# A fused attention and soft-MoE kernel: first q and k turned in the scores' banks, row maxima half a slot later, negated maxima ahead of load issues

## The chip, the cores and the metric

The kernel runs on one core of a Trainium2 chip. The metric is device time in microseconds (us). The engines are named as in the profile: PE (TensorE matmuls, with PEld for its weight loads), DVE (VectorE), ACT (ScalarE), POOL (GpSimd), SP (SyncE). DMAs are issued from GpSimd's queue for all inputs and from SyncE's queue for the output.

## The reference

```python
def _attn_ref(q, k, v):                    # q, k, v: (8, 12, 448, 64)
    scale = 1.0 / np.sqrt(q.shape[-1])
    scores = scale * np.matmul(q, k.transpose(0, 1, 3, 2))
    m = np.max(scores, axis=-1, keepdims=True)
    e = np.exp(scores - m)
    attn = e / (np.sum(e, axis=-1, keepdims=True) + np.exp(-m) + 1e-09)
    return np.matmul(attn, v)

def _moe_ref(x, phi, w1, w2):              # x: (3584, 768), 8 experts of 4 slots, F = 1024
    logits = x @ phi
    d = np.exp(logits - logits.max(0, keepdims=True)); d /= d.sum(0, keepdims=True) + 1e-09
    slot_input = (d.T @ x).reshape(E, S_per_e, D)
    slot_out[e] = np.maximum(slot_input[e] @ w1[e], 0.0) @ w2[e]
    c = np.exp(logits - logits.max(1, keepdims=True)); c /= c.sum(1, keepdims=True) + 1e-09
    return c @ slot_out
```

The attention output, with heads put side by side, is the x of the mixture.

## The kernel before

The 96 heads are worked in 48 pairs (`NPAIR`); a pair is two heads of one batch, on partitions 0 to 63 and 64 to 127. Three pairs (`NP`) are one load group of q, k and v, so there are 16 groups (`NG`). The program order of each engine is written out by hand in one loop over slots `s`, one slot for each pair and one more, each of two half slots `y` (`hs = 2 * s + y`).

The steps of a pair n are these.

- `T(n)` turns q and k: 28 transposes on PE into one PSUM tile `ps_t` (L216), then a copy to SBUF, by ACT (L219) for n < 6 and for the first pair of each group, else by DVE (L221). Seven such copies exist in turn (`NQK`).
- `A(n, i)`, a run, computes a quarter of the pair's scores for the row maxima alone: matmuls into `ps_a` (L249, L259, or L240 where they are mixed with other work) and `reduce_max` on DVE (L253, L262, L242). Runs 0 to 2 have a maximum for each head, run 3 (64 rows a head) one for both, so a pair has seven maxima. The list `runs` holds the order of all runs, and `As(c)` takes the next c of them.
- `W1(g)` negates the maxima of a maxima group on GpSimd (L269: three instructions into `wm`, one into `ngm`). Maxima group 0 is pair 0 alone, group 1 is pairs 1 and 2, later ones are three pairs. `W2(g)` turns them by four matmuls into `ps_m` (L289, L290), `W3(g)` copies that to `mT` and makes the exponentials `ec` of the negated maxima (L295 to L301, ACT).
- `Bk(n, i)` computes the scores again, turned, with keys on partitions, adds the negated maximum by a second matmul with `sel` and `mT`, and ACT takes the exponential (L320 to L325 where a run is mixed in, else L349 to L355).
- `V(g)` puts v of a group into place on GpSimd (four copies, L361 to L364). `AV` multiplies the exponentials with v and a column of ones (L386), `N1` evacuates the sums (L398), `N2` divides by the denominators (`rec`, L407, L408 on DVE, L414 to L423 on GpSimd; on DVE for the last four pairs), and `PX` turns the result for the mixture (L444, L450).
- `P(b)` gives the steps of the mixture's routing for one batch, spread over later half slots by the table `post`.

In slot s the loop runs `Bk(s, ..)`, two runs in each half slot (four in half slots 0 to 4, `early`), `T(s + 6)`, or `T(hs + 3)` in the first half slots, `AV(s, ..)` and the late part of `AV(s - 1, ..)`, `N1` and `N2` of s - 1 and `PX(s - 2)`. In every third slot (s % 3 == 2), in the second half, come W2 and W3 of the next maxima group; W1 of that group stands at the end of the slot before.

PSUM has three pools: `psA` with three banks (tag "a": `ps_a`, `ps_t`, the routing's tiles), `psB` with four (tag "b": `ps_b`, `ps_m`, `ps_x`), `psV` with one.

All loads are issued by GpSimd, in the order of the program: q, k and v of later groups (`load`), half matrices of the experts' weights in two DMAs each (`load_half`, at slots given by `half_at`), and the rows of the last five half matrices (`load_rows`, at half slots given by `rows_at`), which go to SBUF that q, k, v and their products have left by then; rows 7 and 8 go to the place of the loaded v. After the loop come the experts' two layers (L741, L755) and the output (L811 to L822).

Of the kernel before, what the change touches and what calls it, by code (L numbers as in the profile page):

```python
# [9 lines left out]
BF16 = mybir.dt.bfloat16  # L10
# [14 lines left out]
HG = 6  # L25
NP = 3
W65 = 65
# [4 lines left out]
def kernel(  # L32
# [10 lines left out]
    nc = tc.nc  # L43
    B, H, S, D = q.shape
# [9 lines left out]
    NPAIR = B * PB  # L54
    NG = NPAIR // NP
# [69 lines left out]
    def load_rows(r0, r1):  # L125

        while r0 < r1:
            i, z = divmod(r0, FK)
            n = min(r1 - r0, FK - z)
            load_part(11 + i, z, z + n)  # L130
            r0 += n

    with ExitStack() as at:
# [33 lines left out]
        load(1, "k")  # L167


        for h in range(2):  # L170
            nc.vector.tensor_add(ident2[:, 64 * h:64 * h + 64], ident[:, 0:64], ident[:, 64:128])
        nc.vector.tensor_copy(identf, ident)
# [6 lines left out]
                pattern=[[-1, HG]], channel_multiplier=1)  # L179

        nc.vector.reduce_max(band, ident.rearrange("p (i s) -> p i s", i=4), axis=AX.X)
# [11 lines left out]
        nc.vector.memset(ones[64:128, 1:2], 0.0)  # L193
        gdma(out=phi_sb, in_=moe_phi.rearrange("(j p) s -> p j s", p=128))

        mx, ngm, ec, mT, eT, av, us = {}, {}, {}, {}, {}, {}, {}
# [8 lines left out]

        def T(n):
            g, pl = divmod(n, NP)
            ps = psA.tile([128, 2, S], BF16, tag="a", name="ps_t")
            for a in range(2):
                src = nat["qk"[a], g]  # L210
                for tok in range(7):
                    for hl in range(2):

                        c = kcol(hl, tok) if a else (2 * tok if tok < 4 else 2 * tok - 7) * 64
                        r = slice(64 * hl, 64 * hl + 64)
                        nc.tensor.transpose(ps[r, a, c:c + 64], src[r, pl, tok * D:(tok + 1) * D], ident[r, r])  # L216
            t = qk_t[n % NQK]
            if n < 6 or pl == 0:
                nc.scalar.copy(t, ps)  # L219
            else:  # L220
                nc.vector.tensor_copy(t, ps)  # L221
            qkT[n] = t
# [377 lines left out]
            post.setdefault(2 * NPAIR - 5 + 2 * z - (z == 3), []).append(last[z])  # L600


        runs = [(n, i) for n in range(NPAIR) for i in range(4)]

        def As(c):
            for _ in range(min(c, len(runs))):
# [14 lines left out]
        As(1)  # L621
        for nm in "qk":
            load(2, nm)

        half_at = {s: i for i, s in enumerate((1, 4, 7, 10, 13, 16, 22, 25, 28, 31, 34))}


        rows_at = {77: 3, 83: 7, 85: 12, 87: 13, 89: 17, 91: 20, 92: 24, 93: 26, 95: 27}  # L630
        rows = 0
        for s in range(NPAIR + 1):
            for y in range(2):
                hs = 2 * s + y
                early = int(hs < 5)
                mix = s >= 3 and len(runs) > 1 and runs[0][1] == 2 * y
                if mix:
                    Bk(s, 2 * y, mix=True)
                    Bk(s, 2 * y + 1, y, mix=True)
                else:  # L640
                    As(1)
                if mix:
                    pass
                elif s < NPAIR:
                    Bk(s, 2 * y)
                    As(early)
                    side = int(y == 1 and len(runs) > 0 and runs[0][1] == 3)
                    Bk(s, 2 * y + 1, side)
                    As(1 - side)
                else:  # L650
                    As(1)
                if hs == 1:
                    W1(1)
                if hs < 5:
                    T(hs + 3)
                if y == 0:
                    if 0 <= s - 1:
                        for i in (2, 3):
                            AV(s - 1, i, range(3))
                else:  # L660
                    if 2 <= s < NPAIR - 6:
                        T(s + 6)
                    g = (s + 1) // 3
                    if (s + 1) % 3 == 0 and g < NG:
                        W2(g + 1)
                        W3(g + 1)
                    if s < NPAIR:
                        for i in (0, 1):
                            AV(s, i, range(3))
                for f in post.get(hs, ()):  # L670
                    f()
                if y and 0 <= s - 2 < NPAIR - 2:
                    PX(s - 2)
                if y == 0:
                    if 0 <= s - 1:
                        for i in range(4):
                            AV(s - 1, i, [3])
                        if s == NPAIR:
                            PX(s - 2)
                        N1(s - 1)  # L680
                        if not on_pool(s - 1):
                            N2(s - 1)
                else:
                    if 0 <= s - 1 and on_pool(s - 1):
                        N2(s - 1)
                As(early)
                if hs == 1:
                    W2(1)
                    W3(1)
                if hs == 4:  # L690
                    W1(2)
                if y == 0 and hs in rows_at:
                    load_rows(rows, rows_at[hs])
                    rows = rows_at[hs]
            g = (s + 10) // 3
            if s == 1 or (s and s % 3 == 2):
                if g < NG:
                    load(g, "q")
                    load(g, "k")
            g = (s + 9) // 3  # L700
            if s % 3 == 0 and g - 2 < NG:
                V(g - 2)
                if s and g - 1 < NG:
                    load(g - 1, "v")
            if s % 3 == 1:
                if 1 < (s + 2) // 3 < NG:
# [146 lines left out]
```

## Time and profile before

| | |
|---|---|
| median of 3 runs | 311.84 us (311.04 to 312.73) |
| profiled execution | 313.42 us |
| its span, first to last instruction | 311.6 us |
| busy: DVE maxima L242, L262, L253 | 135.3, 29.4, 23.7 us (612 to 617 ns each) |
| busy: ACT copies of T (L219), DVE copies of T (L221) | 18.8 us in 20; 17.1 us in 28 |
| DMA, mean over the span | 174 GB/s |

A row of the timeline has the start in us, the duration, engine, line, operation, result and operands, the count of instructions merged into the row and, in brackets, how long the engine had stood before it and what it waited for last. Where several instructions are merged, the duration is from the first's start to the last's end; an instruction's own duration is a little longer than the distance to the next. A row of the table of stretches has the stretch in us, its length, then for PE, PEld, DVE, ACT and POOL the busy time and count, the clock share, the DMA share and GB/s.

### The profile page before, as it was taken

To read this page: it belongs to the slowest core of one execution; us is meant where nothing else is said; L and a number is where in the kernel's file an instruction comes from. 1 tells how busy PE (TensorE), PEld (TensorE's weight loads), DVE (VectorE), ACT (ScalarE), POOL (GpSimd) and SP (SyncE) were. 2 spreads that over 40 slices of the span, in tenths; PEclk is the share of its full clock that TensorE was granted. 3 is DMA by queue.
4 is the path that set the end of the run, shared out by engine and by line. 5 is a ranking of instruction groups with operands and counts; after the bars stand their busy time and mean duration, and the time that the engine had idled before them with its cause. 6 is when DMAs were issued, how large, how long until landed. Compare 5 with 4: busy or idle time off the path is not lost.

```text
span 311.6 us, 12145 instructions
## 1 busy us (share of the span) xinstructions
PE 279.1 (90%) x5070; PEld 160.7 (52%) x5070; DVE 250.9 (81%) x575; ACT 247.4 (79%) x546; POOL 196.9 (63%) x402
## 2 busy tenths in 40 slices
PE   2899899999999999999999999999999996997800
PEld 1444466565566566656556665566655554461100
DVE  4777999999989999998999899989997455237910
ACT  2357499999999999999899999998999984218700
POOL 8642778879878987697979688976776713000000
PEclk9999999999999999999999999999999998697555
DMA  6990399999999999687999999999445999935997
GB/s 86 150 130 12 45 203 207 198 190 169 190 196 166 208 172 208 78 129 126 207 156 187 171 203 154 194 181 160 79 53 103 161 191 210 211 72 214 449 439 312
DMA packets 36934, 54.30 MB, mean 174 GB/s; under 512 B 2576, under 2 KB 27664, under 8 KB 36496
## 3 DMA queue, kind: packets, MB, share of 16 engines
q0 software_dynamic: 35872, 42.52, 84.8%
q1 hardware_dynamic: 1008, 11.01, 8.3%
q8 instruction: 39, 0.64, 0.8%
q14 instruction: 15, 0.12, 0.1%
HBM read 85.03 MB, written 11.01 MB: 308 GB/s over the span
## 4 chain that ended last, share of the span: by engine, by line
PE 68%; DVE 15%; ACT 6%; issue 3%; POOL 3%; POOLq 0%
PE ps_av L386 14%; PE ps_a L240 10%; PE ps_t L216 7%; PE ps_b L320 6%; DVE mx L242 6%; PE ps_b L323 6%; PE ps_b L349 5%; DVE mx L253 3%; PE ps_b L352 3%; PE ps_o L811 3%; PE ps_x L444 3%; PE ps_h L741 2%; PE ps_a L249 2%; PE ps_s L544 2%; ACT W L817 2%
## 5 line engine op out<-in xcount | busy, mean ns | idle before, releaser
L242 DVE TENSOR_REDUCE mx<-ps_a 128x1 f32<-128x448 f32 x246 | 135.3, 612 | 3.3 <-PE ps_a L240 2.6
L325 ACT ACTIVATE W<-ps_b 128x448 bf16<-128x448 f32 x246 | 118.4, 575 | 0.2 <-PE ps_a L240 0.2
L240 PE MATMUL ps_a<-W 64*128 64x448 bf16 x246 | 79.9, 352 | 0.0
L320 PE MATMUL ps_b<-W 64*128 64x448 bf16 x246 | 67.8, 352 | 0.3
L323 PE MATMUL ps_b<-mT,sel 64*128 64x448 bf16 x246 | 65.5, 350 | 0.0
L386 PE MATMUL ps_av<-W 128*128 128x65 bf16 (+1 forms) x1536 | 65.2, 196 | 0.3 <-issue 0.3
L386 PEld LDWEIGHTS <-W 128*128 128x128 bf16 (+1 forms) x1536 | 50.4, 101 | 27.6 <-issue 23.6
L414 POOL TENSOR_TENSOR W<-ubuf,rec 128x384 bf16<-128x384 f32 x44 | 36.2, 823 | 37.8 <-DVE rec L408 24.3
L355 ACT ACTIVATE W<-ps_b 128x448 bf16<-128x448 f32 x90 | 47.5, 568 | 8.0 <-PE ps_b L352 8.0
L216 PEld LDWEIGHTS <-W 64*64 64x64 bf16 x1344 | 31.2, 113 | 19.2 <-issue 8.0
L216 PE MATMUL ps_t<-ident,W 64*64 64x64 bf16 x1344 | 32.1, 198 | 5.8 <-DMA W<-in_q_dram 4.2
L112 POOL DMA_DIRECT2D W<-in_moe_w_dram x37 | 24.7, 669 | 13.7 <-PE ps_s L544 5.1
L450 ACT CAST W<-ps_x 128x512 bf16<-128x512 f32 x47 | 28.1, 599 | 5.9 <-PE ps_x L444 5.7
L262 DVE TENSOR_REDUCE mx<-ps_a 128x1 f32<-128x448 f32 x48 | 29.4, 613 | 0.6 <-PE ps_a L259 0.3
L349 PE MATMUL ps_b<-W 64*64 64x448 bf16 (+1 forms) x138 | 28.9, 380 | 0.1
L240 PEld LDWEIGHTS <-W 64*128 64x128 bf16 x246 | 23.0, 94 | 9.8
L219 ACT COPY W<-ps_t 128x896 bf16<-128x896 bf16 x20 | 18.8, 940 | 11.3 <-PE ps_t L216 11.1
L253 DVE TENSOR_REDUCE mx<-ps_a 128x1 f32<-128x448 f32 x42 | 23.7, 617 | 4.5 <-PE ps_a L249 4.2
L352 PE MATMUL ps_b<-mT,sel 64*64 64x448 bf16 (+1 forms) x138 | 27.0, 362 | 0.0
L323 PEld LDWEIGHTS <-sel 64*128 64x128 bf16 x246 | 20.0, 94 | 12.4 <-issue 2.2
L398 ACT COPY ubuf<-ps_av 128x455 f32<-128x455 f32 x44 | 25.2, 574 | 1.2 <-PE ps_av L386 1.0
L423 POOL TENSOR_TENSOR W<-ubuf,rec 128x128 bf16<-128x128 f32 x44 | 17.5, 398 | 3.7
(133 smaller groups left out, 440.1 us busy)
## 6 DMA issues: line engine op xcount, KB each, us to landing
W<-in_moe_w_dram POOLq DMA_DIRECT2D x25, 768.0 KB, 9.8
out_dram<-W SPq DMA_DIRECT2D x3, 2688.0 KB, 11.1
W<-in_v_dram POOLq DMA_DIRECT2D x32, 192.0 KB, 6.2
W<-in_q_dram POOLq DMA_DIRECT2D x15, 336.0 KB, 6.6
W<-in_k_dram POOLq DMA_DIRECT2D x15, 336.0 KB, 7.4
W<-in_moe_w_dram POOLq DMA_DIRECT2D x5, 576.0 KB, 10.1
out_dram<-W SPq DMA_DIRECT2D x3, 768.0 KB, 4.2
W<-in_moe_w_dram POOLq DMA_DIRECT2D x1, 960.0 KB, 9.7
```

The source lines that it names most:

```text
L216: nc.tensor.transpose(ps[r, a, c:c + 64], src[r, pl, tok * D:(tok + 1) * D], ident[r, r])
L240: nc.tensor.matmul(ps[:, 0:S], t[r, 0, i * 128:(i + 1) * 128], t[r, 1, :], start=True, stop=True)
L242: nc.vector.reduce_max(m[:, c:c + 1], ps[:, 0:S], axis=AX.X)
L253: nc.vector.reduce_max(mx[g][:, c:c + 1], pss[hl][:, 0:S], axis=AX.X)
L320: nc.tensor.matmul(pss[hl][:, 0:S], t[rs[hl], 1, cols], t[rs[hl], 0, :], start=True, stop=False)
L323: nc.tensor.matmul(pss[hl][:, 0:S], sel[rs[hl], 2 * pl + hl:2 * pl + hl + 1].to_broadcast([64, 128]), mT[mg(n)][rs[hl], :], start=False, s ...
L325: nc.scalar.activation(e[:, hl, :], pss[hl][:, 0:S], AF.Exp, scale=scale)
L349: nc.tensor.matmul(outs[hl], t[rs[hl], 1, cols], t[rs[hl], 0, :], start=True, stop=False)
L352: nc.tensor.matmul(outs[hl], sel[rs[hl], 2 * pl + hl:2 * pl + hl + 1].to_broadcast([64, m]), mT[mg(n)][rs[hl], :], start=False, stop=True)
L355: nc.scalar.activation(e, p[:, 0:S], AF.Exp, scale=scale)
L386: nc.tensor.matmul(o, eT[n, i, hl][:, qc], vp[g % 2][:, 2 * pl + hl, i, 0:W65], start=(i == 0 and u == 0 and hl == 0), stop=(i == 3), skip ...
L414: eng.tensor_mul(x[:, 0:3, c:c + 128].rearrange("p i (h d) -> p i h d", h=2), u[:, 0:6, 0:D].rearrange("p (i h) d -> p i h d", h=2), rec[: ...
```

## The change

- **Setup.** The work on the identity (`ident2`, `identf`, `sel`, `band`) moves behind the memsets on DVE. The order on GpSimd stays.
- **T.** For the first nine pairs `ps_t` is in `psB`. The copy of T(0) is split: q by ACT, k by DVE. The copies of T(7) and T(8) move from DVE to ACT.
- **Runs.** The order in a pair is 0, 3, 1, 2. Half slot 4 takes two runs in place of four, so that all later maxima are taken half a slot later and the last two runs lie in slot 44.
- **W1.** From group 2 on, W1 stands at the end of the first half of the slot in whose second half W2 stands. The order on GpSimd stays, other than in slots 1, 2 and 44.
- **Weight loads.** Half matrix 0 is loaded ahead of the loop, the others a step earlier up to slot 13, then at slots 19, 22, 28, 31 and 34 (before: 16, 22, 25, 28, 31 and 34). The first DMA of a half and `load(2, "v")` stand behind W1.
- **The end.** V(15) moves from the end of slot 42 to slot 44, behind W1(16) and ahead of N2(43), and with it the loads of rows 7 and 8; row 12 is loaded half a slot later.

```diff
         def T(n):
             g, pl = divmod(n, NP)
-            ps = psA.tile([128, 2, S], BF16, tag="a", name="ps_t")
+            first = n < NP * NP
+            ps = (psB if first else psA).tile([128, 2, S], BF16, tag="b" if first else "a", name="ps_t")
...
             t = qk_t[n % NQK]
-            if n < 6 or pl == 0:
+            if n == 0:
+                nc.scalar.copy(t[:, 0, :], ps[:, 0, :])
+                nc.vector.tensor_copy(t[:, 1, :], ps[:, 1, :])
+            elif first or pl == 0:
                 nc.scalar.copy(t, ps)
...
-        runs = [(n, i) for n in range(NPAIR) for i in range(4)]
+        runs = [(n, i) for n in range(NPAIR) for i in (0, 3, 1, 2)]
...
         for nm in "qk":
             load(2, nm)
+        for z in range(2):
+            load_half(0, z, w_tile(0))
-        half_at = {s: i for i, s in enumerate((1, 4, 7, 10, 13, 16, 22, 25, 28, 31, 34))}
+        half_at = {s: i + 1 for i, s in enumerate((1, 4, 7, 10, 13, 19, 22, 28, 31, 34))}
-        rows_at = {77: 3, 83: 7, 85: 12, 87: 13, 89: 17, 91: 20, 92: 24, 93: 26, 95: 27}
+        rows_at = {77: 3, 83: 7, 85: 12, 88: 13, 89: 17, 91: 20, 92: 24, 93: 26, 95: 27}
...
-                early = int(hs < 5)
-                mix = s >= 3 and len(runs) > 1 and runs[0][1] == 2 * y
+                early = int(hs < 4)
+                mix = s >= 3 and len(runs) > 1 and runs[0][1] == 1 - y
...
-                if hs == 4:
-                    W1(2)
+                if y == 0 and s % 3 == 2 and (s + 1) // 3 < NG:
+                    W1((s + 1) // 3 + 1)
+                    if s == 2:
+                        load(2, "v")
+                    if s == NPAIR - 4:
+                        V(NG - 1)
+                        load_rows(7, 9)
+                    if s - 1 in half_at:
+                        load_half(half_at[s - 1], 0, w_tile(half_at[s - 1]))
...
-            if s % 3 == 0 and g - 2 < NG:
+            if s % 3 == 0 and g - 2 < NG - 1:
                 V(g - 2)
...
-            if s % 3 == 1:
-                if 1 < (s + 2) // 3 < NG:
-                    W1((s + 2) // 3 + 1)
-                if s == 1:
-                    load(2, "v")
-            if s in half_at:
-                load_half(half_at[s], 0, w_tile(half_at[s]))
             if s - 1 in half_at:
                 load_half(half_at[s - 1], 1)
             if 2 * s + 1 in rows_at:
-                load_rows(rows, rows_at[2 * s + 1])
+                load_rows(rows + 2 * (rows == 7), rows_at[2 * s + 1])
                 rows = rows_at[2 * s + 1]
```

More of the change, by code (lines that the diff above doesn't have):

```diff
@@ L167 @@
         load(1, "k")
-        for h in range(2):
-            nc.vector.tensor_add(ident2[:, 64 * h:64 * h + 64], ident[:, 0:64], ident[:, 64:128])
-        nc.vector.tensor_copy(identf, ident)
-        nc.gpsimd.memset(sel, 0.0)
-        for base in (0, 64):
-            nc.gpsimd.affine_select(
-                out=sel[base:base + 64], in_=sel[base:base + 64], fill=1.0,
-                compare_op=ALU.not_equal, base=0,
-                pattern=[[-1, HG]], channel_multiplier=1)
-        nc.vector.reduce_max(band, ident.rearrange("p (i s) -> p i s", i=4), axis=AX.X)
         nc.vector.memset(halfm, 0.0)
@@ L193 @@
         nc.vector.memset(ones[64:128, 1:2], 0.0)
+        for h in range(2):
+            nc.vector.tensor_add(ident2[:, 64 * h:64 * h + 64], ident[:, 0:64], ident[:, 64:128])
+        nc.vector.tensor_copy(identf, ident)
+        nc.gpsimd.memset(sel, 0.0)
+        for base in (0, 64):
+            nc.gpsimd.affine_select(
+                out=sel[base:base + 64], in_=sel[base:base + 64], fill=1.0,
+                compare_op=ALU.not_equal, base=0,
+                pattern=[[-1, HG]], channel_multiplier=1)
+        nc.vector.reduce_max(band, ident.rearrange("p (i s) -> p i s", i=4), axis=AX.X)
         gdma(out=phi_sb, in_=moe_phi.rearrange("(j p) s -> p j s", p=128))
```

## The prediction

> **What bounds the kernel now.** I read the page's first two parts, then the table of stretches, then the timeline of the front, of two slots in the middle and of the last score slots.
>
> ```profile
> span 311.6 us, 12145 instructions
> PE 279.1 (90%) x5070; PEld 160.7 (52%) x5070; DVE 250.9 (81%) x575; ACT 247.4 (79%) x546; POOL 196.9 (63%) x402
> ...
> PEclk9999999999999999999999999999999998697555
> ```
>
> ```profile
> 24.00:30.00 6.00, 5.31 (x76) 2.48 (x74) 4.91 (x10) 4.08 (x10) 1.27 (x3) 1.00 0.03 6
> ...
> 42.00:48.00 6.00, 5.88 (x116) 3.52 (x114) 5.53 (x13) 6.00 (x14) 5.61 (x11) 1.00 1.20 208
> ...
> 240.00:246.00 6.00, 5.45 (x88) 2.91 (x85) 1.38 (x8) 5.85 (x15) 4.40 (x12) 1.00 0.73 121
> ```
>
> The columns are PE, PEld, DVE, ACT, POOL. From 42 us on three engines are full (PE 5.88, DVE 5.53, ACT 6.00 of 6 us), so nothing that is only reordered there can gain much. The front is another stage: at 24 to 30 us PE, DVE and ACT all have holes and the DMA rests (0.03). Near 240 us DVE has nearly run dry (1.38 of 6), while ACT is full. The change moves maxima, DVE work, from the front to that last stretch, so the front is what I price.
>
> The transposes T(3) to T(8), one per half slot, are the clock of the front:
>
> ```profile
> 17.39 0.96 PE L216 MATMUL ps_t<-ident,W 64*64 64x64 bf16 x28
> 22.17 0.96 PE L216 MATMUL ps_t<-ident,W 64*64 64x64 bf16 x28
> 27.22 0.63 PE L216 MATMUL ps_t<-ident,W 64*64 64x64 bf16 x28 [0.18 <-DVE mx L262]
> 31.70 0.63 PE L216 MATMUL ps_t<-ident,W 64*64 64x64 bf16 x28 [0.18 <-DVE mx L262]
> 35.93 0.63 PE L216 MATMUL ps_t<-ident,W 64*64 64x64 bf16 x28 [0.18 <-DVE mx L262]
> 39.34 0.63 PE L216 MATMUL ps_t<-ident,W 64*64 64x64 bf16 x28
> ```
>
> Pitches are 4.78, 5.05, 4.48, 4.23 and 3.41 us. Three of these transposes wait for a maximum, because they take one of the three score banks (psA). And 28 transposes take 0.96 us before about 24 us, 0.63 us after, though the clock row shows full speed.
>
> **The change part by part.** The sum is made against the profiled execution: 313.42 us, of which the span is 311.6. The runs' median is 311.84, 1.6 us lower; I carry the difference in us over to it.
>
> *First scores (setup order, T(0)'s split copy).*
>
> ```profile
> 1.88 0.56 POOL L152 DMA_DIRECT2D W<-in_k_dram  x1
> ...
> 3.06 0.29 DVE L171 TENSOR_TENSOR ident<-ident 128x64 bf16<-128x64 bf16 x2 [3.06 <-POOL ident masks.py:199]
> ...
> 4.05 0.56 POOL L152 DMA_DIRECT2D W<-in_q_dram  x1
> 4.21 1.11 PE L216 MATMUL ps_t<-ident,W 64*64 64x64 bf16 x28 [4.21 <-DMA W<-in_q_dram]
> 5.37 0.91 ACT L219 COPY W<-ps_t 128x896 bf16<-128x896 bf16 x1 [3.35 <-PE ps_t L216]
> 6.33 0.93 PE L249 MATMUL ps_a<-W 64*128 64x448 bf16 x3 [1.01 <-ACT W L219]
> 7.04 0.06 DVE L193 MEMSET ones<- 64x1 bf16 x1
> 7.13 2.22 DVE L253 TENSOR_REDUCE mx<-ps_a 128x1 f32<-128x448 f32 x4
> ```
>
> DVE idles 3.06 us for the identity, then sets up without a gap until 7.1 us and takes the first maximum at once: setup, not the score, sets 7.13. The memsets need no identity and can now go first; 4.07 us of setup (3.06 to 7.13) that begins by 1.3 us, an estimate from GpSimd's issues that run by 1.88, ends by 5.4. The copy of T(0) is cut in two on two engines: 448 columns on ACT cost 0.53 us (the mT copy at 40.31, below) in place of 0.91, so the scores start near 5.95 in place of 6.33, and a maximum follows its matmul by 0.59 (9.23 to 9.82, below): 6.54 against 7.13, a gain of 0.6 us. Bounds: 0 (if DVE's setup begins late) to 0.8.
>
> A rule of the Trainium skill speaks against this step: SBUF — State Buffer, "Who interferes with whom", says that a VectorE copy or cast in a two-port mode holds a port pair that GpSimd needs for the descriptors of its DMAs, and blocks it for the whole instruction. The trace does not agree for the memsets: an issue takes 0.56 us while DVE is idle (1.88) and 0.56 beside setup (4.05). By the rule, one 0.29 us operation ahead of an issue would turn this gain of 0.6 into 0.3.
>
> *T in the scores' other pool (psB) for nine pairs.* No instruction is added. The waits that it can remove stand in these rows:
>
> ```profile
> 9.23 0.70 PE L249 MATMUL ps_a<-W 64*128 64x448 bf16 x2
> ...
> 9.82 1.16 DVE L253 TENSOR_REDUCE mx<-ps_a 128x1 f32<-128x448 f32 x2 [0.47 <-PE ps_a L249]
> ...
> 13.76 2.21 DVE L253 TENSOR_REDUCE mx<-ps_a 128x1 f32<-128x448 f32 x4 [0.96 <-PE ps_a L249]
> ...
> 17.50 1.16 DVE L253 TENSOR_REDUCE mx<-ps_a 128x1 f32<-128x448 f32 x2 [0.60 <-PE ps_a L249]
> ```
>
> DVE stands 2.0 us in these three. A bank no longer sits under T from its first transpose to the end of ACT's copy, so scores run one bank further ahead. The 0.47 is of that kind entirely. The 0.96 stands partly behind the first W2, which waits for GpSimd, and stays in part. I take 1.2, bounds 0 and 2.0. The price is in psB: T takes one of the four banks of the exponentials' scores. It is hidden as long as ACT, which stands idle about 1 us four times from 31 to 39 us, empties them in time; if not, each T waits for one exponential (about 0.5 us).
>
> *Two runs fewer in half slot 4, copies of T(7), T(8) on ACT.* With hs < 4 the front computes 26 runs before slot 3 in place of 28: four maxima fewer between T(6) and T(8), and two copies leave DVE.
>
> ```profile
> 33.13 2.22 DVE L253 TENSOR_REDUCE mx<-ps_a 128x1 f32<-128x448 f32 x4
> ...
> 36.86 0.61 DVE L221 COPY W<-ps_t 128x896 bf16<-128x896 bf16 x1
> ```
>
> ```profile
> 32.37 0.91 ACT L219 COPY W<-ps_t 128x896 bf16<-128x896 bf16 x1 [0.72 <-PE ps_t L216]
> 34.40 1.94 ACT L355 ACTIVATE W<-ps_b 128x448 bf16<-128x448 f32 x4 [1.12 <-PE ps_b L352]
> 37.32 0.54 ACT L398 COPY ubuf<-ps_av 128x455 f32<-128x455 f32 x1 [0.98 <-PE ps_av L386]
> 38.93 1.42 ACT L355 ACTIVATE W<-ps_b 128x448 bf16<-128x448 f32 x3 [1.08 <-PE ps_b L352]
> 40.31 0.53 ACT L295 CAST mT<-ps_m 128x448 bf16<-128x448 f32 x1
> ```
>
> DVE would save 2.2 + 2 x 0.61 = 3.4 us. But ACT inherits two copies of 0.91. From T(6) at 31.70 to the copy of mT, which slot 3 waits for, 8.61 us pass now. ACT's work in that stretch becomes 0.91 + 1.94 + 0.91 + 0.54 + 1.42 + 0.91 = 6.63, and it starts 0.67 after T(6): 7.30. So ACT takes the bound over from DVE and the gain is 1.3 us; bounds 0 (a wait at each step stays) and 3.4. After mT the order on ACT is what it was, so the gain is carried on.
>
> *Maxima half a slot later, W1 half a slot later, in every third slot.* The order on GpSimd in the middle is unchanged, but W1 (four negations) now needs the maxima of its own slot's first half. On DVE nothing is added. Queued behind W1 are a weight load's issue, and N2 (the multiplies by rec); PE waits for W1 at W2.
>
> ```profile
> 152.41 2.22 DVE L242 TENSOR_REDUCE mx<-ps_a 128x1 f32<-128x448 f32 x4 [0.29 <-PE ps_a L240]
> ...
> 154.33 0.97 POOL L269 TENSOR_SCALAR W<-mx 128x36 bf16<-128x36 f32 x3
> ...
> 156.31 0.34 PE L289 MATMUL ps_m<-ident,W 128*128 128x128 bf16 x3
> ```
>
> The four maxima end at 154.63, so W1 would start near 154.8 in place of 154.33 and end its three negations near 155.8, 0.5 us ahead of W2. Cost 0; bounds 0 and, if DVE ran one maximum later (2.22 / 4 = 0.55), a few tenths per group.
>
> *Weight loads.* The first half matrix is loaded in two issues ahead of the loop; later ones shift. The two issues (0.56 each in the nearest rows) lie ahead of W1(1) on GpSimd, which stands idle then, and their transfers fall into the DMA's hole at 24 to 30 us. Cost 0, at most 1.1.
>
> *The end.* Four maxima and their matmuls move into slot 44; V(15)'s copies move behind W1(16), ahead of N2(43).
>
> ```profile
> 238.03 0.66 POOL L361 COPY W<-W 128x576 bf16<-128x576 bf16 x1
> ...
> 239.76 0.34 POOL L364 COPY W<-W 64x192 bf16<-64x192 bf16 x1
> ...
> 243.18 0.97 POOL L269 TENSOR_SCALAR W<-mx 128x36 bf16<-128x36 f32 x3
> ...
> 243.54 0.34 PE L289 MATMUL ps_m<-ident,W 128*128 128x128 bf16 x3 [0.23 <-POOL W L269]
> ...
> 245.91 0.82 POOL L414 TENSOR_TENSOR W<-ubuf,rec 128x384 bf16<-128x384 f32 x1 [0.98 <-ACT W L450]
> ...
> 248.86 0.40 PE L444 MATMUL ps_x<-ident,W 128*128 128x128 bf16 x4
> ```
>
> The maxima sit on an idle DVE, their matmuls beside a full ACT: 0 to 0.5. W2's wait for the late W1 (0.23) goes. But V(15) takes 2.1 us (238.03 to 240.10). After W1 ends near 243.8 come these copies and three issues of about 0.56: N2(43) starts near 247.6 in place of 245.91 and ends 1.5 later, 0.3 after PX(43)'s place at 248.86. I take +0.5 for the end, bounds -0.2 and +1.5.
>
> Sum: -0.6 - 1.2 - 1.3 + 0 + 0.5 = -2.6 us. The profiled execution would be 310.8, the median 309.2.
>
> **The rivals.**
>
> *The clock comes sooner.* Before about 24 us PE runs slow, and pitches are 4.78 and 5.05 against 4.23 later. If a denser front lets PE speed up before T(3), these two lose 0.55 and 0.82: 1.4 us more, 307.8. For it: PE's holes shrink. Against: it stayed slow from 4.21 to past 22.17 us, through five sets of transposes and the scores between them. TensorE: Matmul & The Clock Gate in the Trainium skill, Part 1, says that one busy window of about 3.4 us releases half rate; the rows agree with two rates, not with so short a wait.
>
> *The gain is given back.* The copies on ACT and the fuller psB hold T(6) to mT at 8.6 us, and the end takes 1.2: 311.84 - 0.6 - 1.2 + 1.2 = 311.2. For it: ACT is full right after (6.00 of 6). Against: ACT's holes before 40.31 sum to 3.9 us in the rows shown.
>
> *W2 waits in every group (slower).* Place: PE at W2, once in three slots, 14 times. It decides once the fourth maximum ends less than 1.2 us ahead of W2's place (0.97 for W1, some 0.2 for two hand-overs); today 1.7 us at 156.31. If the maxima lagged by two more (1.1 us), each group would stand 0.6: 8.4 us, less the 2.6: 317.6; by 1.5 of them, 0.3 each, 4.2: 313.4. For it: DVE is as full as PE, 5.53 of 6. Against: three score banks let DVE lag by three maxima only.
>
> **How the numbers follow.** Forecast 0.52 (own range 308.0 to 310.4), clock 0.13, given back 0.22, slower 0.13. A measurement of this kernel can tell about 0.5%, 1.6 us, from no change: faster means under 310.3, slower over 313.4. From the forecast 0.47 is faster, with the clock case 0.60; the given-back case and the forecast's edge make 0.25 the same; the slower case and an end worse than bounded make 0.15. The range is 307.2 to 312.8: low by the clock case and a little more than 1.2 from the banks, high by the given-back case with its end at the bound.
>
> **What would show it.** First maximum near 6.5 us and no wait of T for a maximum; T(4) near 20.3; mT of slot 3 near 37.2; ACT without holes from T(6) on; W2 in the middle without a wait for W1; from there every stage 3.1 us early; a wait of PX(43) for N2 and the DMA's end unchanged relative to the hidden layers. Wrong would be: W2 waiting for the negations in the middle, a front that is early at T(3) and not at slot 3, or an end that takes over 1.5 us.

## The result, and the profile after

| | before | changed |
|---|---|---|
| median of the runs, us (5 each) | 311.84 (311.04 to 312.73) | 309.65 (309.09 to 310.31) |
| profiled execution, us | 313.42 | 309.65 |
| its span, us | 311.6 | 307.8 |

The ratio of changed to before is 0.9913, 95% interval 0.9885 to 0.9942. The forecast was 309.2, range 307.2 to 312.8. The time fits, but the parts of the sum do not; most of what follows is about that.

Starts of the same work in the two profiled executions, in us from the start of the span:

| work | before | changed | earlier by |
|---|---|---|---|
| first maximum | 7.13 | 6.95 | 0.2 |
| T(3) | 17.39 | 15.51 | 1.9 |
| T(6) | 31.70 | 27.36 | 4.3 |
| copy of mT for slot 3 | 40.31 | 34.47 | 5.8 |
| W2 shown at 156.31 | 156.31 | 150.55 | 5.8 |
| W2(16) | 243.54 | 237.78 | 5.8 |
| PX(43) | 248.86 | 243.08, stands 0.77 inside | 5.8 |
| PX(44) | 253.66 | 248.70 | 5.0 |
| first hidden layer | 266.16 | 261.13 | 5.0 |
| first output matmul | 281.84 | 277.98 | 3.9 |

The front won almost twice what was forecast (3.1), the middle kept all of it, and the end gave 1.9 back, where 0.5 was forecast.

The transposes T(3) to T(8) in the timeline of the changed kernel (start, duration, engine, line, operation; T's line is now 217), with two pairs of score matmuls (L263) that show TensorE's rate (of T(3) the row of its first 22 transposes):

```profile
12.11 0.58 PE L263 MATMUL ps_a<-W 64*64 64x448 bf16 x2
...
15.51 0.77 PE L217 MATMUL ps_t<-ident,W 64*64 64x64 bf16 x22
...
16.07 0.38 PE L263 MATMUL ps_a<-W 64*64 64x448 bf16 x2
...
19.06 0.63 PE L217 MATMUL ps_t<-ident,W 64*64 64x64 bf16 x28
...
23.11 0.63 PE L217 MATMUL ps_t<-ident,W 64*64 64x64 bf16 x28
...
27.36 0.63 PE L217 MATMUL ps_t<-ident,W 64*64 64x64 bf16 x28
...
30.29 0.63 PE L217 MATMUL ps_t<-ident,W 64*64 64x64 bf16 x28
...
32.64 0.60 PE L217 MATMUL ps_t<-ident,W 64*64 64x64 bf16 x28
```

No transpose waits for a maximum any more. TensorE's rate changes during T(3), near 16 us: the same pair of score matmuls takes 0.58 at 12.11 and 0.38 at 16.07, and from T(4) on 28 transposes take 0.63. Before, it changed between 23 and 24 us. The pitch from T(3) to T(5) is 7.60, against 9.83.

The stretches that the prediction opened with (columns PE, PEld, DVE, ACT, POOL, granted clock, DMA):

```profile
24.00:30.00 6.00, 5.77 (x84) 2.58 (x81) 5.53 (x13) 4.09 (x8) 0.90 (x2) 1.00 1.08 204
...
42.00:48.00 6.00, 6.00 (x128) 3.56 (x124) 5.73 (x13) 5.83 (x14) 5.03 (x12) 1.00 1.20 208
240.00:246.00 6.00, 5.17 (x79) 2.64 (x79) 3.46 (x10) 5.10 (x13) 5.31 (x10) 1.00 0.80 110
```

In the front PE goes from 5.31 to 5.77 and DVE from 4.91 to 5.53 of 6 us, so that both are now nearly full; the middle looks as before; near 240 us it is POOL that has filled up (4.40 to 5.31).

### The profile page after: what moved, and what is told of

Same layout as the page of the kernel before. It is cut to its first block, busy times and chain, and to the rows that moved or that the text cites. A ratio compares the mean times of both kernels' runs of the same rounds, so it can differ in the third digit from the quotient of the medians.

```text
span 307.8 us, 12143 instructions
## 1 busy us (share of the span) xinstructions
PE 275.8 (90%) x5070; PEld 159.8 (52%) x5070; DVE 250.3 (81%) x574; ACT 248.2 (81%) x548; POOL 198.3 (64%) x403
## 4 chain that ended last, share of the span: by engine, by line
PE 61%; DVE 14%; ACT 7%; DMA 5%; issue 4%; POOL 3%; POOLq 0%; DVEq 0%; ACTq 0%
PE ps_av L390 14%; PE ps_a L244 9%; DVE mx L246 8%; PE ps_t L217 7%; PE ps_b L324 6%; PE ps_b L327 6%; DMA W<-in_moe_w_dram 4%; PE ps_b L353 4%; PE ps_b L356 3%; PE ps_x L448 2%; PE ps_a L253 2%; ACT W L824 2%; DVE mx L257 2%; PE ps_o L818 2%; PE ps_s L548 2%
## 5 line engine op out<-in xcount | busy, mean ns | idle before, releaser
L244 PE MATMUL ps_a<-W 64*128 64x448 bf16 x250 | 81.1, 351 | 0.0
L324 PE MATMUL ps_b<-W 64*128 64x448 bf16 x250 | 69.0, 352 | 0.4 <-ACT W L223 0.2
L327 PE MATMUL ps_b<-mT,sel 64*128 64x448 bf16 x250 | 66.4, 350 | 0.1
L418 POOL TENSOR_TENSOR W<-ubuf,rec 128x384 bf16<-128x384 f32 x44 | 36.4, 827 | 34.9 <-ACT W L454 13.9
L217 PEld LDWEIGHTS <-W 64*64 64x64 bf16 x1344 | 30.3, 112 | 17.9 <-issue 6.9
L353 PE MATMUL ps_b<-W 64*64 64x448 bf16 (+1 forms) x134 | 26.9, 374 | 0.2
L223 ACT COPY W<-ps_t 128x896 bf16<-128x896 bf16 x21 | 19.9, 946 | 6.9 <-PE ps_t L217 6.5
L356 PE MATMUL ps_b<-mT,sel 64*64 64x448 bf16 (+1 forms) x134 | 25.1, 356 | 0.2
L427 POOL TENSOR_TENSOR W<-ubuf,rec 128x128 bf16<-128x128 f32 x44 | 17.9, 407 | 3.7
```

The lines of the kernel that those rows point to most:

```text
L244: nc.tensor.matmul(ps[:, 0:S], t[r, 0, i * 128:(i + 1) * 128], t[r, 1, :], start=True, stop=True)
L324: nc.tensor.matmul(pss[hl][:, 0:S], t[rs[hl], 1, cols], t[rs[hl], 0, :], start=True, stop=False)
L327: nc.tensor.matmul(pss[hl][:, 0:S], sel[rs[hl], 2 * pl + hl:2 * pl + hl + 1].to_broadcast([64, 128]), mT[mg(n)][rs[hl], :], start=False, s ...
L353: nc.tensor.matmul(outs[hl], t[rs[hl], 1, cols], t[rs[hl], 0, :], start=True, stop=False)
L356: nc.tensor.matmul(outs[hl], sel[rs[hl], 2 * pl + hl:2 * pl + hl + 1].to_broadcast([64, m]), mT[mg(n)][rs[hl], :], start=False, stop=True)
L418: eng.tensor_mul(x[:, 0:3, c:c + 128].rearrange("p i (h d) -> p i h d", h=2), u[:, 0:6, 0:D].rearrange("p (i h) d -> p i h d", h=2), rec[: ...
```

## Experiments

Each kernel was run beside the kernel before on one chip, and its ratio is to that. Two chips were used, so kernels are compared with each other by ratio.

**The end: V(15) back where it was.** Timeline of the changed kernel, GpSimd, the two matmul groups that wait, and the experts' first layer (L748):

```profile
238.01 0.66 POOL L365 COPY W<-W 128x576 bf16<-128x576 bf16 x1
...
239.80 0.35 POOL L368 COPY W<-W 64x192 bf16<-64x192 bf16 x1
240.44 1.69 POOL L112 DMA_DIRECT2D W<-in_moe_w_dram  x3 [0.30 <-POOL W L368]
242.20 0.83 POOL L418 TENSOR_TENSOR W<-ubuf,rec 128x384 bf16<-128x384 f32 x1
...
243.39 0.74 POOL L427 TENSOR_TENSOR W<-ubuf,rec 128x128 bf16<-128x128 f32 x1
...
244.19 0.23 PE L448 MATMUL ps_x<-ident,W 128*128 128x128 bf16 x1 [0.77 <-POOL W L427]
...
261.13 6.10 PE L748 MATMUL ps_h<-W,ubuf 128*32 128x512 bf16 x72
...
274.57 1.95 PE L762 MATMUL ps_so<-W 128*32 128x384 bf16 x41 [0.72 <-DMA W<-in_moe_w_dram]
```

Four copies of V(15) and three issues stand ahead of N2(43) (L418 to L427), which ends at 244.13; the last matmul of PX(43) has waited 0.77 for it. Thirty us later the experts' second layer (L762; the expectations call it the score slots) waits 0.72 for the last weights; before, it ran its 96 matmuls without a wait (276.28 to 280.36).

```diff
                     if s == NPAIR - 4:
-                        V(NG - 1)
-                        load_rows(7, 9)
...
-            if s % 3 == 0 and g - 2 < NG - 1:
+            if s % 3 == 0 and g - 2 < NG:
                 V(g - 2)
...
-                load_rows(rows + 2 * (rows == 7), rows_at[2 * s + 1])
+                load_rows(rows, rows_at[2 * s + 1])
```

> The changed kernel with V(15) and rows 7, 8 back at the end of slot 42, the rest as changed. Theory: in the changed kernel PX(43) stands 0.77 us for N2(43), which is queued behind V(15) and three issues, and the last experts' matmuls stand 0.72 us for the last weights, whose loads came later. Put back, V(15) fits into the 1.84 us that GpSimd stood idle ahead of N2(42); both waits go, and the time is 308.2 us (309.65 for the changed kernel). Rival: V(15) makes W1(16) late again and W2 waits for it, or the end of the loads does not move: 309.6 us.

Measured: 307.40, ratio 0.9844 (0.9799 to 0.9889). The same places:

```profile
232.82 0.66 POOL L365 COPY W<-W 128x576 bf16<-128x576 bf16 x1
...
235.20 1.16 POOL L112 DMA_DIRECT2D W<-in_moe_w_dram  x2 [0.30 <-POOL W L368]
...
241.89 0.40 POOL L427 TENSOR_TENSOR W<-ubuf,rec 128x128 bf16<-128x128 f32 x1
...
243.65 0.40 PE L448 MATMUL ps_x<-ident,W 128*128 128x128 bf16 x4
...
261.03 5.27 PE L745 MATMUL ps_h<-W,ubuf 128*32 128x512 bf16 x72
...
270.47 4.08 PE L759 MATMUL ps_so<-W 128*32 128x384 bf16 x96
```

N2(43) now ends 1.4 us ahead of PX(43), the first of the last loads is issued 5 us earlier, and both waits are gone. The rival came in part: W1(16) is late again, and W2(16) starts at 238.34 in place of 237.78, its last matmul after a wait of 0.32 for W1. So the experts' first layer starts only 0.1 earlier than in the changed kernel (261.03). The span is 2.0 shorter all the same: 1.0 is the second layer's, and 0.8 the first layer's, whose 72 matmuls ran 5.27 in place of 6.10. There the granted clock is 0.50 at first and rises on the way; from 264 to 267 us it was 1.00 here and 0.79 in the changed kernel. Nothing shows that this 0.8 comes from the edit: over the fourteen profiles of this case these matmuls ran from 4.36 to 6.32 us.

To tell the copies from the loads, V(15) alone went back, and the load of rows 7 and 8 stayed with W1(16):

```diff
                     if s == NPAIR - 4:
-                        V(NG - 1)
                         load_rows(7, 9)
...
-            if s % 3 == 0 and g - 2 < NG - 1:
+            if s % 3 == 0 and g - 2 < NG:
```

> The changed kernel with V(15) alone back at the end of slot 42; the load of rows 7 and 8 stays with W1(16). Theory: the copies of V(15), 2.1 us of GpSimd ahead of N2(43), are what made PX(43) wait (0.77) and what held the following loads back so that the score slots waited for the last weights (0.72): both waits go, span 306, time 307.5 to 308. Rival: the three loads' issues (1.7 us) ahead of N2(43) matter as much: PX(43) keeps 0.3 to 0.7 of its wait or the score slots keep theirs, time 308.7 to 309.6.

Measured: 307.70, ratio 0.9855 (0.9828 to 0.9883), span 304.8. PX(43) starts at 242.95 and does not wait; the second layer runs on without a wait for weights, although three issues still stand ahead of N2(43). So the 2.1 us of copies made PX(43) wait, and the issues alone are hidden. PX(43) waits 0.60 to 0.77 in all four profiles that have V(15) in slot 44, and in none of the ten others.

The wait for the last weights is less clear. It comes in two of these four (0.72, and 0.77 with T in psA). The two others, with the runs back and with the copies of T(7) and T(8) on VectorE (both below), have the same copies and issues there, and their second layer takes 4.1 us to the next step without that wait. So the copies alone do not bring it, and what else it takes stays open.

**The pool of T, alone.** The kernel before with T(0) to T(8) in psB:

```diff
-            ps = psA.tile([128, 2, S], BF16, tag="a", name="ps_t")
+            first = n < NP * NP
+            ps = (psB if first else psA).tile([128, 2, S], BF16, tag="b" if first else "a", name="ps_t")
```

> The kernel before with one edit: T of the first nine pairs in psB. Theory: the bank under T is what opens the front: T(3) near 16 us in place of 17.39, the 28 transposes at 0.63 us from T(4) on, mT of slot 3 near 38.0 in place of 40.31, time 310.0 us. Rival: the two runs fewer are what counts: T(3) at 17.2, transposes slow until 24 us, mT near 40, time 311.7 us.

Measured: 310.92, ratio 0.9949 (0.9916 to 0.9982). mT of slot 3 at 37.57, 2.7 earlier, but T(3) at 17.00, hardly earlier. Most of the gain comes after T(3): the rate rises between 18 and 19 us in place of 23 to 24, and T(3) to T(5) take 7.92 (17.00 to 24.92) in place of 9.83.

**Everything but the pool.** The changed kernel with T in psA:

```diff
-            ps = (psB if first else psA).tile([128, 2, S], BF16, tag="b" if first else "a", name="ps_t")
+            ps = psA.tile([128, 2, S], BF16, tag="a", name="ps_t")
```

> The changed kernel with one edit undone: every T in psA. Theory: the waits of T for maxima return, PE stays slow until about 24 us, and mT of slot 3 comes near 37.0 us in place of 34.47; time 311.5 us. Rival: two runs fewer carry the gain: mT near 35.0, time 310.0 us.

Measured: 311.18, ratio 0.9954 (0.9930 to 0.9978); five of the transposes T(1) to T(8) wait for maxima again (0.18 to 0.19 each), mT at 36.46. Beside the other parts the pool is thus worth 2.0 us at mT (36.46 to 34.47). But the expected slow rate until 24 us did not come: it rose at 17.0. So something else in the change thickens the front, too.

**The runs back.** What is left is the list of runs: the change takes them in the order 0, 3, 1, 2 and computes two fewer in half slot 4. Both undone:

```diff
-        runs = [(n, i) for n in range(NPAIR) for i in (0, 3, 1, 2)]
+        runs = [(n, i) for n in range(NPAIR) for i in range(4)]
...
-                early = int(hs < 4)
-                mix = s >= 3 and len(runs) > 1 and runs[0][1] == 1 - y
+                early = int(hs < 5)
+                mix = s >= 3 and len(runs) > 1 and runs[0][1] == 2 * y
```

> The changed kernel with 28 runs ahead of slot 3 as before in place of 26, in the order 0, 1, 2, 3; T stays in psB, T(7) and T(8) are copied by ACT. My prediction's term: two runs fewer (four maxima, 2.2 us of VectorE) are part of the 1.3 us between T(6) and mT, together with the two copies that left VectorE. Theory A (ACT is the bound there, and VectorE has room: it idles 1.0 us between 31 and 35 us in the change): the four maxima cost 0.6 to 1.2 us, mT at 35.1 to 35.7, time 310.2 to 310.8. Theory B (VectorE is the bound): all of 2.2 us, mT at 36.7, time 311.5. Third outcome: no cost, mT at 34.5, then the shift of runs brings nothing in the front.

Measured: 312.96, ratio 1.0011 (0.9988 to 1.0034): the gain in time is gone. mT came at 38.15, later than either theory allowed, though still 2.2 ahead of the kernel before. The runs spread from 311.58 to 314.09; the profiled one, 311.74, has a span of 310.0, which is 1.6 under that of before, so the median and the profile do not agree on what is left. Its transposes T(1), T(3) and T(6):

```profile
8.11 0.96 PE L217 MATMUL ps_t<-ident,W 64*64 64x64 bf16 x28
...
16.86 0.96 PE L217 MATMUL ps_t<-ident,W 64*64 64x64 bf16 x28
...
29.08 0.63 PE L217 MATMUL ps_t<-ident,W 64*64 64x64 bf16 x28
```

The number of runs differs in half slot 4 alone, behind T(6). What is lost up to T(6), 1.7 us (29.08 against 27.36), is therefore the order's. The kernel before with the pool alone has T(6) at 29.14, so up to there the pool (2.6 of 31.70 to 27.36) and the order (1.7) are all that the change won. A further 2.0 lie between T(6) and mT (9.07 against 7.11); there both the number and the order of the runs differ, and they were not tried apart. Why the order matters can be read in the first scores, in the changed kernel and then with the runs back:

```profile
6.38 0.55 PE L253 MATMUL ps_a<-W 64*128 64x448 bf16 x2 [1.05 <-DVE W L221]
6.87 0.58 PE L263 MATMUL ps_a<-W 64*64 64x448 bf16 x2
6.87 0.96 PE L217 MATMUL ps_t<-ident,W 64*64 64x64 bf16 x28
```

```profile
7.65 0.53 PE L253 MATMUL ps_a<-W 64*128 64x448 bf16 x1 [0.34 <-DVE mx L257]
```

Run 0 takes two banks of psA, run 3 (L263) only one. In this order three banks hold both runs, and T(1) follows at 6.87; in the order 0, 1 the fourth matmul waits for the first maximum (0.34, until 7.65) and T(1) stands behind it until 8.11. That the later pairs gain by the same mechanism is argued from this, not shown.

**Copies of T(7) and T(8) back on VectorE.**

```diff
-            elif first or pl == 0:
+            elif n < 6 or pl == 0:
```

> The changed kernel with the copies of T(7) and T(8) back on VectorE. My prediction's term: ACT is the bound from T(6) to mT, so with 1.82 us of copies off ACT and 1.22 on VectorE that stretch, 7.1 us in the changed kernel (27.36 to 34.47), should become shorter or stay: mT at 34.0 to 34.5, time 309.3 to 309.7. Rival: VectorE is still the bound there even with two runs fewer; then mT comes 0.6 to 1.2 us later, 35.1 to 35.7, and the time is 310.3 to 310.8.

Measured: 308.49, ratio 0.9878 (0.9839 to 0.9918). mT at 33.68, 0.8 earlier than in the changed kernel, more than expected. ACT's timeline from T(8)'s neighbourhood to mT, first the changed kernel, then this one:

```profile
31.18 0.94 ACT L223 COPY W<-ps_t 128x896 bf16<-128x896 bf16 x1
31.97 0.59 ACT L402 COPY ubuf<-ps_av 128x455 f32<-128x455 f32 x1
32.40 1.48 ACT L359 ACTIVATE W<-ps_b 128x448 bf16<-128x448 f32 x3
33.69 0.99 ACT L223 COPY W<-ps_t 128x896 bf16<-128x896 bf16 x1
34.47 0.64 ACT L299 CAST mT<-ps_m 128x448 bf16<-128x448 f32 x1
```

```profile
31.65 0.54 ACT L402 COPY ubuf<-ps_av 128x455 f32<-128x455 f32 x1 [0.35 <-PE ps_av L390]
32.38 1.42 ACT L359 ACTIVATE W<-ps_b 128x448 bf16<-128x448 f32 x3 [0.18 <-PE ps_b L356]
33.68 0.54 ACT L299 CAST mT<-ps_m 128x448 bf16<-128x448 f32 x1
```

In the changed kernel ACT has no hole from 30 us on, and the copy of T(8) stands directly ahead of mT. So ACT is the bound there, and the copies on it cost 0.8 us at mT. By the time alone the two kernels are not told apart (the changed one's interval is 0.9885 to 0.9942).

**The first scores.** T(0) copied in one piece by VectorE, with V(15) and rows 7, 8 back as above:

```diff
             if n == 0:
-                nc.scalar.copy(t[:, 0, :], ps[:, 0, :])
-                nc.vector.tensor_copy(t[:, 1, :], ps[:, 1, :])
+                nc.vector.tensor_copy(t, ps)
```

> The same without the dense matmuls: the change, V(15) and rows 7 and 8 back, T(0) copied whole by VectorE in one piece (0.61 us from 5.35) in place of two halves of which VectorE's started 1.0 late. Theory: the first scores start at 6.0 in place of 6.38 and the first maximum at 6.6 in place of 6.95; 0.3 us under the run with V(15) back alone (ratio to before 0.984), so a ratio of 0.983. Rival: the next wait (T(1) for its load, the later maxima) takes it: ratio 0.984 to 0.985.

Measured: 308.08, ratio 0.9871 (0.9826 to 0.9917), not told apart from 0.9844 without this edit. First the changed kernel's copies, then this one's start and its T(3):

```profile
5.37 0.53 ACT L220 COPY W<-ps_t 128x448 bf16<-128x448 bf16 x1 [3.36 <-PE ps_t L217]
...
5.94 0.39 DVE L221 COPY W<-ps_t 128x448 bf16<-128x448 bf16 x1 [1.03 <-ACT W L220]
...
6.95 1.16 DVE L257 TENSOR_REDUCE mx<-ps_a 128x1 f32<-128x448 f32 x2 [0.62 <-PE ps_a L253]
```

```profile
5.25 0.63 DVE L220 COPY W<-ps_t 128x896 bf16<-128x896 bf16 x1 [0.34 <-PE ps_t L217]
5.93 0.56 PE L252 MATMUL ps_a<-W 64*128 64x448 bf16 x2 [0.72 <-DVE W L220]
...
6.52 1.16 DVE L256 TENSOR_REDUCE mx<-ps_a 128x1 f32<-128x448 f32 x2 [0.64 <-PE ps_a L252]
...
15.10 0.47 PE L217 MATMUL ps_t<-ident,W 64*64 64x64 bf16 x14
...
15.93 0.31 PE L217 MATMUL ps_t<-ident,W 64*64 64x64 bf16 x8 [0.36 <-DMA W<-in_k_dram]
```

The two halves run one after the other, 0.96 us together (5.37 to 6.33), where one copy by VectorE takes 0.63. Why VectorE's half was held until ACT's was done was not tried apart. With the whole copy the first maximum comes 0.4 earlier, as expected. But T(3) then waits 0.36 in its middle for k of the next group, and T(4) is back at 19.02 (19.06 in the changed kernel), mT at 34.44 (34.47): at T(3) a transfer is the next limit, as the rival had it.

**TensorE's rate.** Three fillings with matmuls whose results nobody reads. Seven on zeros ahead of T(0), in the kernel before (the memset of their operand `wm` moves ahead on VectorE for it):

```diff
+        warm, flat0 = pb_("ps_warm"), wm[0].rearrange("p i c -> p (i c)")
+        for _ in range(7):
+            nc.tensor.matmul(warm, wm[0][:, 0, :], flat0, start=True, stop=True)
         T(0)
```

> The kernel before with seven matmuls on a zeroed tile on PE ahead of T(0), in the 4.2 us in which PE waits for the first q and k; their output is not used. Theory: a large part of the front's gain is that PE runs at full rate from 15.6 us on in place of 24: with full rate from the start the pitches T(3) to T(5) fall from 4.78 and 5.05 to about 4.3, mT of slot 3 comes near 38.0 in place of 40.31, time 309.6 us. Rival: DVE's maxima bound the front at either rate: mT near 39.8, time 311.4 us. A third outcome: the rate does not rise with these matmuls, and nothing changes.

Measured: 313.17, ratio 1.0025 (1.0000 to 1.0050). The third outcome came: T(0) to T(4) still took 0.96 to 1.01, and the rate rose at about 23.5 us, as without the matmuls; mT came at 39.81. The matmuls ran from 1.19 to 4.36 and T(0) to 5.30, 4.1 us without a hole. Then a longer filling up to T(1), on ones, where `fill(k)` is k such matmuls (again a memset of `wm` moves ahead):

```diff
+        fill(7)
         T(0)
-        As(2)
+        fill(2)
+        As(1)
+        fill(1)
+        As(1)
         T(1)
```

> The kernel before, with seven 128x512 matmuls on a tile of ones ahead of T(0), two behind it and one between the first two runs, so that TensorE has no hole from 1.2 us to the end of T(1). Theory: the rate rises once TensorE has worked without a hole for long enough; in the runs so far it rose 3.6 to 4.5 us after the last hole (before: dense from 19.9, fast by 23.8; T in psB: from 14.1, by 19.1; the change with psA: from 12.5, at 17.0; the change: from 11.6, at 16.1). The seven matmuls on zeros with T(0) were dense for 4.1 us only, too near to that. Here it is dense for over 7 us, so T(1) or T(2) at the latest takes 0.63, T(3) and T(4) are fast, the pitches before T(4) and T(5) fall from 4.78 and 5.05 to near 4, mT of slot 3 comes at 38.0 in place of 40.3, and the time is 2 us under the kernel before, near 310.3. Rival: the rise hangs on something else (the time since the start, the amount of real work, many score matmuls): T(0) to T(4) stay at 0.96, mT at 40, time 312.5 to 313.

Measured: 310.78, ratio 0.9950 (0.9919 to 0.9981); the time and mT (38.07) came near, the course did not. T(1) and T(2), and three stretches with the granted clock (third column from the end):

```profile
8.31 0.63 PE L216 MATMUL ps_t<-ident,W 64*64 64x64 bf16 x28 [0.18 <-DVE mx L253]
11.04 0.95 PE L216 MATMUL ps_t<-ident,W 64*64 64x64 bf16 x28 [0.21 <-DVE mx L262]
```

```profile
7.00:11.00 4.00, 3.27 (x39) 1.32 (x38) 3.90 (x8) 0.91 (x1) 2.60 (x7) 0.97 1.22 157
11.00:17.00 6.00, 5.78 (x62) 2.45 (x63) 4.37 (x9) 3.18 (x8) 5.58 (x13) 0.50 1.01 123
18.00:24.00 6.00, 5.32 (x71) 2.38 (x72) 5.58 (x11) 4.14 (x10) 3.15 (x10) 1.00 0.93 128
```

The rate was up at T(1), fell at 10.8 us after a stretch in which TensorE was busy 3.27 of 4 us, stayed at half from 11 to 17 and rose again at 17.6, in place of 23 to 24. T(3) to T(5) took 8.35 (16.63 to 24.98) in place of 9.83: 1.5 us for the rate. The profiled execution, 313.41, was the slowest of the ten. Of the 2.2 us that it has won at mT, 0.3 are left at W2(16) (243.24); holes of 0.67 up to 98.5 us and 0.55 up to 124.4, in which TensorE waits for nothing that the profile shows, are part of this.

The same filling in the changed kernel, with V(15), rows 7 and 8 back and T(0) copied by VectorE (the diffs above put together):

> The changed kernel with V(15) and the load of rows 7 and 8 back at the end of slot 42, T(0) copied whole by VectorE, and nine dense matmuls on ones ahead of T(0), behind it, and one between the first runs. Theory: everything is fast from T(2) at the latest in place of 16.1 us; in the stretch from 7 to 16 us VectorE's maxima (0.55 each) set the pace, so little more comes of it: T(3) at 14.8 against 15.5, mT of slot 3 at 33.7 against 34.5, time 0.5 to 1 us under the next run. Rival: rate unchanged, time as the next run.

Measured: 308.11, ratio 0.9880 (0.9814 to 0.9946), nothing beside 0.9871 without it. mT came at 34.91 in place of 33.7: the clock fell to 0.50 here too, from 10.0 to 16.8 us. The holes were then filled up to T(2), beyond the filling shown above, in a kernel with V(15), rows 7, 8 and the copies of T(7), T(8) back; that kernel (the two diffs put together) was run without filling as well:

> The changed kernel with V(15) and the load of rows 7 and 8 back at the end of slot 42, and the copies of T(7) and T(8) on VectorE. Each alone gave a ratio to before of 0.984 and 0.988, against 0.991 for the change. Theory: the two lie in different stages and add up: mT of slot 3 at 33.7 (34.5 in the change), no wait of PX(43) and none for the last weights; ratio 0.981 to 0.982, 306.6 us. Rival: the 0.8 us won in the front is lost again at the end, where GpSimd or the last weights become the bound: ratio 0.984.

```diff
         T(1)
-        As(2)
+        As(1)
+        fill(2)
+        As(1)
+        fill(2)
         W1(0)
...
         As(1)
+        fill(2)
         T(2)
```

> The first kernel of this call with dense matmuls on ones ahead of and behind T(0), and two behind each of the first four runs, until T(2). With fewer of them (nine and one) the rate rose at 6.5 to 7 us and the granted clock fell to 0.5 at 10 to 11 us, after a stretch of some 3 us in which TensorE had holes (busy 0.69 to 0.82 of each us), until 16.5 to 17.7. Theory: it is those holes that shut the clock again; with them filled, T(1) to T(4) all take 0.63, the clock row shows no slice under 9 in the first 60 us, and T(4), 19.06 in the change, comes 0.5 to 1.5 us earlier, time 0.5 to 1 us under the first kernel. Rival: it falls all the same, as by a limit on what the core may draw: T(2) or T(3) at 0.96 and 0.5 in the clock row, time equal to or up to 1.5 us over the first kernel.

Measured: without filling 307.50, ratio 0.9837 (0.9808 to 0.9867), mT at 33.70; with it 306.88, ratio 0.9827 (0.9801 to 0.9853), mT at 33.41. T(0) behind the same seven matmuls on ones, first with the shorter filling, then with the longer one:

```profile
4.55 0.96 PE L217 MATMUL ps_t<-ident,W 64*64 64x64 bf16 x28
```

```profile
4.55 0.69 PE L217 MATMUL ps_t<-ident,W 64*64 64x64 bf16 x28
```

The front with the longer one:

```profile
7.00:11.00 4.00, 3.95 (x52) 1.24 (x54) 4.00 (x9) 0.91 (x1) 2.62 (x7) 1.00 1.09 131
11.00:17.00 6.00, 4.88 (x85) 2.34 (x80) 5.42 (x12) 4.27 (x10) 5.65 (x13) 1.00 1.11 136
```

```profile
10.83 0.63 PE L217 MATMUL ps_t<-ident,W 64*64 64x64 bf16 x28
...
15.68 0.31 PE L217 MATMUL ps_t<-ident,W 64*64 64x64 bf16 x8 [0.58 <-DMA W<-in_k_dram]
```

The clock stays at 1.00, T(1) and T(2) take 0.63, and it is worth only 0.3 us at mT: DVE is busy 4.00 of 4 us from 7 to 11, and then T(3) waits 0.58 for its k. That the filled holes are what kept the clock up is not shown: the rate rose earlier here from the start (T(0) at 0.69), and from 11 to 17 us TensorE was busy only 4.88 of 6 us without a fall. The two times are not told apart. The two edits of the kernel without filling, 0.984 and 0.988 alone, do not visibly add up in the times either (0.9837), though its profiled execution has the hidden layers at 259.74 (261.03 with V(15) back alone) and the shortest span, 304.4. Both kernels beat the changed one: their intervals lie below its 0.9885.

## Why the prediction was right, and where its steps were not

- *What bounds.* Right: the front had the room, the middle none. All of the 5.8 us won by slot 3 is still there at W2(16).
- *First scores, -0.6: mis-sized, -0.2.* VectorE's setup did end early (at 4.9 us, and the issues beside its memsets and a cast took 0.55 to 0.57 as when it idled, so the port rule of the Trainium skill's SBUF — State Buffer, "Who interferes with whom", was not seen at work here), and ACT's half took 0.53 as written. The step that failed is "the scores start near 5.95": the halves were taken as parallel, but VectorE's waited 1.03, until ACT's was done, and the scores started at 6.38. By T(6) none of the 0.2 is left: the pool and the order account for all that was won there.
- *Pool, -1.2 with bounds 0 and 2.0: mis-sized, at the bound.* The mechanism held (no T waits for a maximum, no T for an exponential). It was worth 2.0 beside the other parts and 2.7 alone, and of the 2.7 alone 1.9 lie between T(3) and T(5), where the rate rises sooner. The prediction had put this into the clock rival and priced the waits alone. That the removed waits are what lets the rate rise sooner is argued, not shown.
- *Two runs fewer, copies on ACT, -1.3: right in size for what it names.* T(6) to mT took 7.11, forecast 7.30, with ACT as the bound. With the runs back, in number and order, it is 9.07; with the copies on VectorE it is 6.35. So the runs give 2.0, and the copies on ACT, which the prediction counted among DVE's savings, cost 0.8.
- *The order of the runs: not priced at all, and the largest omission.* The prediction treated 0, 3, 1, 2 as part of the later maxima. It gives 1.7 us by T(6). Without the order and the two fewer runs the time is that of the kernel before (ratio 1.0011), although 2.2 us are still won at mT.
- *W1 half a slot later, 0: right.* Its negations at 148.92 end at 149.89, 0.7 ahead of W2 at 150.55 (0.5 forecast); no W2 in the middle waits for it. The slower rival did not come.
- *The end, +0.5 with bounds -0.2 and +1.5: mis-sized, +1.9.* The place and cause were right (V(15) ahead of N2(43), PX(43) waiting). N2(43) ended 1.05 after PX(43)'s start, not 0.3 after it: everything on TensorE came 5.8 earlier, while W1(16) ahead of V(15) still waited for its maxima. This half cost 0.8 by PX(44). The second half was excluded by the list of what would show it ("the DMA's end unchanged relative to the hidden layers"): the experts' second layer, waiting for weights, took 5.06 us to the next step (271.39 to 276.45) in place of 4.02 (4.01 with V(15) back). That wait came in two of the four profiles with V(15) in slot 44, so its cause is shown in part only.
- *The clock rival, at 0.13: came true in its mechanism.* "It stayed slow through five sets of transposes" was read as inertia, but the work counts too: with the holes ahead of T(1) filled, the rate was up at T(1). Its price, 1.4, agrees with the 1.5 measured in the kernel before. In the changed front it can't be added to the other terms, since VectorE and the k loads bind there.

The number came out by luck, because errors cancelled: the front won 5.8 in place of 3.1, the end lost 1.9 in place of 0.5. The profiled spans differ by 3.8 (2.6 forecast), the medians by 2.2. The difference of the two is the 1.6 by which the profiled execution of before lay above its median, which the prediction carried over as if the changed kernel's would do the same; that one lay at its median. In the sum, 2.7 us more from the front met 1.4 more lost at the end and 1.6 that did not carry over.

## What to carry to other kernels

Price every line of a diff that reorders work, even one that looks like a renumbering: which item takes how many buffers, and what then queues behind the first that has to wait. Where a front is sped up by several us, ask of each job that was moved near the end not only who waits for it in its old place, but who will wait when all else comes that much earlier, and which loads are issued behind it. A filler that keeps an engine's clock up is worth something only if that engine sets the pace.

## What the runs showed of the hardware that was not expected

- TensorE's early slow stretch does not show in the clock row: it reads 1.00 from the start, while 28 transposes take 0.96 us. Only after a first rise is a fall shown (0.50 from 10.8 to 17.6 us above, with T(2) at 0.95). The durations of equal work are the surer reading.
- The moment at which the rate first rises does not follow from the work ahead of it alone. Behind the same seven matmuls on ones, begun at 1.45 us, it rose during T(0) in one execution (0.69 from 4.55), near 6.4 us in another (T(0) 0.96, the first scores 0.40 at 6.41) and between 7.0 and 8.3 in a third (T(0) 0.95, a matmul of 128x512 still 0.56 at 7.00, T(1) 0.63 at 8.31). After 4.1 us of matmuls on zeros and T(0) it did not rise. TensorE: Matmul & The Clock Gate in the Trainium skill, Part 1, gives a window of about 3.4 us that runs free of the kernel; by that a burst of 4.1 us can miss holding a whole window, and the rows agree. Whether the zeros played a part was not tried apart.
- The busy share does not tell when the rate changes. In the changed kernel TensorE counts as busy 3.99 of 4 us from 7 to 11 us and without a hole from there to 16, and the rate rose only near 16. It fell after 3.27 of 4 us busy in the filled kernel before, so no idle stretch is needed to lose it, and it stayed up with 4.88 of 6 us in the last kernel.
- In all fourteen profiles the granted clock falls to 0.50 ahead of the experts' first layer and rises again inside it, in the changed kernel at 258.5 and 265.3 us. With the moment of the rise its 72 matmuls ran from 4.36 to 6.32 us, which is as much as most of the effects above.
- In nine of the fourteen profiles TensorE stands 0.26 to 1.39 us right ahead of the same W2 (at 210.21 in the changed kernel, after 0.41), waiting for nothing that the profile shows. The 1.39 are in the kernel with T(0) copied whole. Single runs of one kernel lie up to 4 us apart (309.22 to 313.41 for the filled kernel before); how much of that is such holes or the clock is not known, since one execution of each is profiled.
